# Softmax maxima from pairs of PSUM banks: one 1024-key reduction in place of two of 512 keys

## The chip, the cores and the metric

The kernel runs on one core of one Trainium2 chip. The metric is device time in microseconds (us) for one execution of the whole program, loads and stores included. Three executions of the kernel before took 2044.47, 2052.12 and 2060.83 us, so the median is 2052.12 us.

Five engines matter, each with its own queue worked in order: TensorE (PE in the profile; its weight loads are listed as PEld), VectorE (DVE), ScalarE (ACT), GpSimd (POOL) and SyncE (SP), which here only starts transfers. Matrix products land in PSUM, which holds eight banks of 512 float32 values per partition. Engines wait for each other through semaphores.

## What is computed

Two attention layers over one sequence of 2048 rows of width 512, 32 heads of 16, and a gated sum of the two:

```
q, k, v = split(x @ wqkv)                       # layer A: every row attends to all 2048 rows
a = softmax(q k^T / 4) v @ wo
# layer B: four segments of 512 rows; inside a segment causal attention,
# between segments a running memory (phi(x) = x+1 for x > 0, else exp(x))
p = softmax(q_s k_s^T / 4 + mask); a_dot = p v_s
a_mem = (phi(q_s) M) / (phi(q_s) z + 1e-6)
M = M + phi(k_s)^T v_s ; z = z + sum(phi(k_s))
b = (sigmoid(beta) a_mem + (1 - sigmoid(beta)) a_dot) @ wo_B
out = g * a + (1 - g) * b ,  g = sigmoid(sum(x * gate_w))
```

The softmax needs the maximum of each row of scores. The kernel computes those maxima exactly, in a pass of their own, before it computes the scores that go into the exponential.

## The kernel before

**Stages.** The first stage projects x to q, k and v of both layers (`qk_tile`, `v_tiles`, tiles `pr`) and builds B's memory (`mem_q`, `mem_k`). Then comes the main loop over 512 steps of layer A and 128 steps of layer B, and after it a tail that finishes the last output rows. A unit is (layer, group of 4 heads, chunk of 512 query rows). A unit of A has 16 steps, one for each block of 128 keys, a unit of B has 4. B's steps have 512, 384, 256 and 128 query columns, because of the causal mask.

**A step of the main loop** emits four score products (`score_parts`, L579, into tiles `st`, three banks; one bank holds one head, or two heads when they have at most 256 columns), the exponentials on ACT (L582), and the products with v of an earlier step (`values`, L601, into the one bank `ops`; in A they come in two halves, so that a step has two half steps). Beside them it emits the maxima of a unit that comes 22 steps later (in B 12 to 20): `max_parts`. In A each step has four products of 128 queries by 512 keys (L197, tiles `sm`), and after each one a maximum on DVE (L199, out to `pm`). A score product and a maximum product use different rows of the array and run side by side. In B a step has 4 products of 512 or of 384 keys, one to a bank, or 4 of 256 or of 128, two to a bank (L210); DVE adds the mask in place and takes the maximum (L215, one custom operation and one that reads its accumulator).

**Behind a unit's last maximum,** `finish_max` joins the partial maxima (`nm`, L162 on DVE; L164 in B), splits them into two parts on POOL (L168, L169), and three steps later `transpose_max` transposes them on PE (L175, tile `mt_ps`), copies them on ACT (L177) and sends them by DMA into the rows 48 and 49 of the q tile, where the score products pick them up.

**Beside the main loop** run the reciprocals of the softmax sums (L623 on DVE, four to a group), their loads and stores, and, in B, the output products: `out_products` (L747, tile `fin`) multiplies finished rows by the output weights. 24 products of 512 columns make one block of 128 output rows; they are hung on the ends of the steps of B in groups of three to five (`filler`). The copy L750 on ACT empties `fin`, and a DMA stores the rows.

**PSUM before.** `sm_ps` has three single banks for the whole program. In the main loop there are beside it three `st` banks, one `ops` bank and one bank `ms_ps`, which takes A's transpositions and, in B, `fin`; B's transpositions take their turn among the `sm` banks.

**Order.** The order of the instructions on every engine is the order in which the Python code emits them (`manual_schedule`). The framework adds the semaphore waits, from the tiles that an instruction reads and writes.

Of the kernel before, what the change touches and what calls it, by code (L numbers as in the profile page):

```python
# [10 lines left out]
F32 = mybir.dt.float32  # L11
F32R = mybir.dt.float32r
AF = mybir.ActivationFunctionType
ALU = mybir.AluOpType
AX = mybir.AxisListType
PSUM = bass.MemoryType.PSUM
# [3 lines left out]
D = 512  # L20
H = 32
DH = 16
CH = 512
# [17 lines left out]
def gated_mix(ctx, tc, x, xT, wqkv, a_wo, b_wq, b_wk, b_wv, b_wo, beta, gate_w, out):  # L41
    nc = tc.nc
# [55 lines left out]
    qp = ctx.enter_context(tc.tile_pool(name="qp", bufs=6))  # L98
    kp = ctx.enter_context(tc.tile_pool(name="kp", bufs=1))
    mp = ctx.enter_context(tc.tile_pool(name="mp", bufs=2))  # L100
    sm_ps = ctx.enter_context(tc.tile_pool(name="sm_ps", bufs=3, space=PSUM))

    units = [("A", g, c) for g in range(NG) for c in range(NCH)]
    units += [("B", g, c) for c in range(NCH) for g in range(NG)]
# [4 lines left out]
    nA = NG * NCH * 16  # L109

    qt, kt_, ktr = {}, {}, {}
# [8 lines left out]
    for i in range(8):  # L120
        t = kp.tile([128, 2, CH], F32R, name=f"k{i}")
# [28 lines left out]
    def rows(t, h, n):  # L150

        return t[64 * (h // 2):64 * (h // 2) + n, h % 2]


    pmt = {}
# [13 lines left out]
        nc.gpsimd.tensor_sub(ms[:, :, 1], nv, ms[:, :, 0].bitcast(F32))  # L169
        return ms  # L170

    def transpose_max(u, ms, pool, tag):

        pt = pool.tile([128, CH], F32, tag=tag, name="mt_ps")
        nc.tensor.matmul(pt[:32, :128], ms.rearrange("p r a h s -> p (r a h s)"), identr, start=True, stop=True)  # L175
        mt = mp.tile([32, 128], F32R, tag="mt", name="mt")
        nc.scalar.copy(mt, pt[:32, :128])  # L177
        for r in range(2):
            nc.sync.dma_start(raw(qt[u])[64 * r + 48:64 * r + 50], raw(mt)[16 * r:16 * r + 16])

    def max_parts(m):

        u, i = steps[m]
        side, g, c = u
        if i == 0:
            pmt[u] = mp.tile([128, 4, 4, 4 if side == "A" else 1], F32, tag="pm" + side, name="pm")
        pm = pmt[u]
        q = qt[u]

        share = {}  # L190

        def part(j):
            if side == "A":

                ps = sm_ps.tile([128, CH], F32, tag="sm", name="sm")
                h, s, kc = (2 if j < 2 else 0) + i // 8, i // 2 % 4, 2 * (i % 2) + j % 2
                nc.tensor.matmul(ps, rows(q[:, :, s * 128:(s + 1) * 128], h, 48), rows(kt_[side, g, kc], h, 48),  # L197
                                 start=True, stop=True)
                nc.vector.tensor_reduce(pm[:, h, s, kc:kc + 1], ps, axis=AX.X, op=ALU.max)  # L199
                return  # L200

            s = 3 - i
            n = (s + 1) * 128
            per = 2 if n <= 256 else 1
            h = (2, 3, 0, 1)[j]
            if j % per == 0:
                share["ps"] = sm_ps.tile([128, CH], F32, tag="sm", name="sm")
            ps = share["ps"]
            n0 = j % per * n
            nc.tensor.matmul(ps[:, n0:n0 + n], rows(q[:, :, s * 128:(s + 1) * 128], h, 48),  # L210
                             rows(kt_[side, g, c][:, :, :n], h, 48), start=True, stop=True)
            if j % per == per - 1:
                for e in range(per):
                    r = ps[:, e * n:(e + 1) * n]
                    nc.vector.tensor_tensor_reduce(r, r, cmask[:, CH - n:], 1.0, -3.0e38, ALU.add, ALU.max,  # L215
                                                   pm[:, h - per + 1 + e, s, 0:1])
        return [lambda j=j: part(j) for j in range(4)]
# [4 lines left out]
            ms = finish_max(u)  # L222
            late.append((m + LATE_T, u, ms))

    def run_late(pool, tag, every=False):
        for e in [e for e in late if every or e[0] < mnext[0]]:
            late.remove(e)
            transpose_max(e[1], e[2], pool, tag)

    loaded = [0]  # L230

# [16 lines left out]
    with ExitStack() as p0:  # L248
# [6 lines left out]
        st = p0.enter_context(tc.tile_pool(name="st", bufs=1))  # L255
        pr_ps = p0.enter_context(tc.tile_pool(name="pr_ps", bufs=3, space=PSUM))
        me_ps = p0.enter_context(tc.tile_pool(name="me_ps", bufs=2, space=PSUM))

# [209 lines left out]
        def some_max(place):  # L470
            if not parts:
                if mnext[0] == LEAD_A:
                    return
                loads(mnext[0] + PRE)
                parts.extend(max_parts(mnext[0]))

            parts.pop(0)()
            parts.pop(len(parts) // 2)()
            if not parts:
                after_max(mnext[0])  # L480
                mnext[0] += 1
                run_late(me_ps, "me")

        s0 = now[0]
        for k in range(NCH):
# [37 lines left out]
    hl = ctx.enter_context(tc.tile_pool(name="hl", bufs=2, reuse_waits="tile"))  # L523
    st_ps = ctx.enter_context(tc.tile_pool(name="st_ps", bufs=3, space=PSUM, reuse_waits="tile"))
    o_ps = ctx.enter_context(tc.tile_pool(name="o_ps", bufs=1, space=PSUM, reuse_waits="tile"))
    ms_ps = ctx.enter_context(tc.tile_pool(name="ms_ps", bufs=1, space=PSUM, reuse_waits="tile"))

    ops = o_ps.tile([128, CH], F32, name="ops")
    nc.vector.memset(ops, 0.0)
# [84 lines left out]
    held = {}  # L614
# [120 lines left out]
            eng.tensor_sub(l[:, os], t, held["hi", side, c, b][:, os].bitcast(F32))  # L735
        held["lo", side, c, b] = l

    def out_products(c, b, n0, n1, pool, tag):
        if n0 == 0:
            held["ps", c, b] = pool.tile([128, D], F32, tag=tag, name="fin")  # L740
        ps = held["ps", c, b]
        for n in range(n0, n1):
            side = "AB"[n // 12]
            half, o = n % 12 // 4, n % 4
            l = held["lo" if half == 0 else "hi", side, c, b]
            r = wos[side][1 if half == 1 else 0]
            nc.tensor.matmul(ps, l[:, o], r[:, o], start=(n == 0), stop=(n == 23))  # L747
        if n1 == 24:
            t = fr.tile([128, D], F32, tag="res", name="res", bufs=2)
            nc.scalar.copy(t, ps)  # L750
            nc.sync.dma_start(out[c * CH + b * 128:c * CH + (b + 1) * 128, :], t)
# [13 lines left out]
    for c in range(1, NCH):  # L765
        t0 = 24 * c
# [21 lines left out]
    def filler(t, f):  # L788
        fill.setdefault(t, []).append(f)

    for c in range(NCH - 1):
        base = nA + (c + 1) * 32
        apart = 7 if c < NCH - 2 else 5
        per = -(-24 // apart)
        at(base + 3, lambda c=c: b_invert_load(c))
        for i in range(4):
            at(base + 6 + i // 2, lambda c=c, i=i: recip(("B", c), i))
        at(base + 7, lambda c=c: b_invert(c))
        for i, os in enumerate(((0, 1), (2, 3))):
            at(base + 6 + i, lambda c=c, os=os: raw_load(c, os))  # L800
            at(base + 8 + i, lambda c=c, os=os: am_load(c, os))
            at(base + 10 + i, lambda c=c, os=os: inv_load(c, os))
            at(base + 12 + i, lambda c=c, os=os: at_load(c, os))
        for b in range(4):
            t0 = base + 14 + apart * b
            at(t0, lambda c=c, b=b: out_mul(c, b))
            at(t0 + 1, lambda c=c, b=b: out_add(c, b))
            at(t0 + 2, lambda c=c, b=b: out_hi(c, b, "B"))
            at(t0 + 3, lambda c=c, b=b: (out_lo(c, b, "B", nc.gpsimd), out_hi(c, b, "A")))
            at(t0 + 4, lambda c=c, b=b: out_lo(c, b, "A", nc.gpsimd))  # L810
            for n in range(24):
                filler(t0 + 5 + n // per, lambda c=c, b=b, n=n: out_products(c, b, n, n + 1, ms_ps, "ms"))


    nS = len(steps)
# [6 lines left out]
    for t in range(nS):  # L822
        for f in beside.get(t, []):
            f()
        side = steps[t][0][0]

        ms_list = []
        while mnext[0] < nS and mnext[0] - lead(mnext[0]) <= t:
            ms_list.append(mnext[0])
            mnext[0] += 1  # L830
        mm = []
        for m in ms_list:
            loads(m + PRE)
            mm += max_parts(m)
        ss = score_parts(t)
        per = -(-len(mm) // 4) if mm else 0
        waiting.append(t)
        lag = LAG_A if side == "A" else LAG_B

        done = [w for w in waiting if w <= t - lag]  # L840
        del waiting[:len(done)]
        for h in range(4):
            for w in done if side == "A" and h == 2 else []:
                values(w, 0)
            for w in done if side == "B" and h == 3 else []:
                values(w)
            ss[h]()
            for f in mm[h * per:(h + 1) * per]:
                f()
        for w in done if side == "A" else []:  # L850
            values(w, 1)
        for m in ms_list:
            after_max(m)

        run_late(*((ms_ps, "ms") if t < nA else (sm_ps, "sm")), every=not ms_list)
        for f in fill.get(t, []):
            f()
    for t in waiting:
# [10 lines left out]
    for b in range(4):  # L869
        out_hi(c, b, "A")  # L870
        out_lo(c, b, "A", nc.vector)
        out_products(c, b, 0, 12, *((sm_ps, "sm") if b < 3 else (st_ps, "st")))
    for b in range(5):
        if b < 4:
            out_mul(c, b)
            out_add(c, b)
            out_hi(c, b, "B")
        if b:
            out_lo(c, b - 1, "B", nc.vector)
            out_products(c, b - 1, 12, 24, None, None)  # L880


def build():
# [32 lines left out]
```

## Time and profile before

| | |
|---|---|
| executions, median (lowest to highest) | 2052.12 us (2044.47 to 2060.83) |
| profiled execution: time, span of its instructions | 2040.8 us, 2039.1 us |
| mean granted TensorE clock in it | 0.953 of full speed |
| busy in the span: PE, DVE, ACT, POOL | 2001.6, 1688.3, 1478.2, 212.0 us |
| main loop, layer A's steps | from about 335 to 1630 us |
| main loop, layer B's steps | from about 1630 to 1998 us |

The profile is of one execution, on its slowest core, which here is the only one. A line "L199 DVE ..." is a group of instructions of line 199 of the program. Out <- in are the program's tile names, the number after x is the count; behind it stand the busy time in us and the mean duration of one in ns. Because instructions overlap on an engine, the busy time of a group can be less than count times mean. "Idle before" is what the engine idled just before these instructions, with the work that ended the idling. Matmuls are pipelined and their ends are modelled, so that PE can read as busy while it isn't at its peak; start to start distances are the safer reading. PEclk is the share of the TensorE clock that was granted.

### The profile page before, as it was taken

The page shows a single profiled execution, that of the slowest core. Times are in us where ns is not written, and L with a number is a line of the kernel's source. Part 1 is how long each engine was busy: PE and PEld are TensorE (multiplying, and loading weights), DVE is VectorE, ACT ScalarE, POOL GpSimd, SP SyncE. Part 2 cuts the span into 40 slices and gives each one's busy share as a digit, 9 for nine tenths or more (in the row PEclk, how much of TensorE's full clock was granted, in tenths as well). Part 3 has the DMA queues.
Part 4 walks back from the last instruction along what each step waited for, and adds up shares of the span by engine and source line. Part 5 has one row for each costly group of instructions (what it writes and reads, how often), then busy time and mean ns, then how long its engine had stood idle before and what let it go on. Part 6 is the DMA issues. An engine that isn't in the chain of part 4 may idle for free.

```text
span 2039.1 us, 41498 instructions
## 1 busy us (share of the span) xinstructions
PE 2001.6 (98%) x16113; PEld 912.9 (45%) x16113; DVE 1688.3 (83%) x3476; ACT 1478.2 (72%) x2823; POOL 212.0 (10%) x372
## 2 busy tenths in 40 slices
PE   8999999999999999999999999999999999999998
PEld 6887665333333333333333333333333344454545
DVE  3235896999999899999999999999998567787842
ACT  3234334888888788888888888888888855565652
POOL 3000000021200100000010000010000023343330
PEclk9999999999999899999999999999999955698989
DMA  6667434032400410110221111130103144546542
GB/s 225 216 232 241 166 141 150 31 100 94 138 15 26 93 44 26 38 35 26 59 66 39 30 30 38 32 94 15 38 15 75 54 121 138 150 146 180 163 132 91
DMA packets 94725, 190.69 MB, mean 94 GB/s; under 512 B 15888, under 2 KB 30000, under 8 KB 91712
## 3 DMA queue, kind: packets, MB, share of 16 engines
q1 hardware_dynamic: 93536, 187.30, 30.6%
q8 instruction: 127, 2.08, 0.4%
q0 software_dynamic: 992, 0.74, 0.2%
q14 instruction: 70, 0.57, 0.1%
HBM read 111.94 MB, written 74.86 MB: 92 GB/s over the span
## 4 chain that ended last, share of the span: by engine, by line
PE 86%; DVE 5%; DMA 4%; ACT 3%; issue 1%; SPq 1%; DVEq 0%; ACTq 0%
PE st L579 35%; PE ops L601 31%; PE pr L274 12%; PE fin L747 4%; DVE pm L199 3%; PE sm L197 2%; ACT p L582 2%; PE sm L210 2%; DMA qA<-mt 1%; ACT oraw L608 1%; DVE sm L215 1%; PE num L422 1%; DMA inv<-rdB 1%; PE mt_ps L175 1%; SPq L694 0%
## 5 line engine op out<-in xcount | busy, mean ns | idle before, releaser
L582 ACT ACTIVATE p<-st 128x512 f32<-128x512 f32 (+2 forms) x2432 | 1298.2, 585 | 301.0 <-PE sm L210 120.8
L199 DVE TENSOR_REDUCE pm<-sm 128x1 f32<-128x512 f32 x2048 | 1254.5, 684 | 31.2 <-PE sm L197 25.1
L579 PE MATMUL st<-qA,k 50*128 50x512 f32 x2048 | 751.4, 447 | 7.7 <-DMA qA<-mt 4.8
L197 PE MATMUL sm<-k,qA 48*128 48x512 f32 x2048 | 751.6, 451 | 0.7 <-DVE pm L199 0.5
L601 PE MATMUL ops<-p,vA 128*17 128x256 f32 x8176 | 645.5, 388 | 5.7 <-ACT oraw L608 5.6
L579 PEld LDWEIGHTS st<-qA,k 50*128 50x128 f32 x2048 | 303.4, 185 | 433.2 <-ACT p L582 411.2
L215 DVE CUSTOM_DVE_ANT_0 sm<-sm,cmask 128x256 f32<-128x256 f32 (+3 forms) x512 | 244.0, 512 | 104.7 <-PE sm L210 81.4
L197 PEld LDWEIGHTS sm<-k,qA 48*128 48x128 f32 x2048 | 310.6, 185 | 24.9 <-DVE pm L199 12.4
L601 PEld LDWEIGHTS ops<-p,vA 128*17 128x17 f32 x8176 | 135.7, 95 | 367.6 <-issue 347.4
L210 PE MATMUL sm<-k,qB 48*128 48x256 f32 (+3 forms) x512 | 183.7, 446 | 5.3 <-DVE pm L215 2.8
L579 PE MATMUL st<-qB,k 50*128 50x256 f32 (+3 forms) x512 | 174.0, 441 | 0.8 <-ACT p L582 0.2
L579 PEld LDWEIGHTS st<-qB,k 50*128 50x128 f32 x512 | 100.4, 235 | 133.5 <-issue 63.1
L168 POOL CAST ms<-nm 128x16 fp32r<-128x16 f32 x64 | 14.1, 220 | 1200.3 <-DVE nm L162 1150.0
L601 PE MATMUL ops<-p,vB 128*17 128x512 f32 (+3 forms) x1024 | 121.6, 556 | 0.0
L323 DVE TENSOR_TENSOR q<-pr,q 128x512 fp32r<-128x512 f32 x64 | 44.0, 687 | 88.0 <-ACT q L316 84.7
L210 PEld LDWEIGHTS sm<-k,qB 48*128 48x128 f32 x512 | 101.8, 233 | 14.7 <-DVE pm L215 9.8
L584 POOL TENSOR_SCALAR_AFFINE_SELECT p<-p 128x512 f32<-128x512 f32 x128 | 82.8, 647 | 244.2 <-ACT p L582 244.2
L316 ACT CAST q<-pr 128x512 fp32r<-128x512 f32 x64 | 37.4, 585 | 82.8 <-PE pr L274 65.6
L215 DVE DVE_READ_ACCUMULATOR2_ANT pm<- 128x1 f32 x512 | 72.2, 141 | 0.1
L274 PE MATMUL pr<-xh,wql 128*128 128x512 f32 x128 | 55.5, 434 | 8.0 <-ACT xh L367 6.0
L274 PE MATMUL pr<-xl,wqh 128*128 128x512 f32 x128 | 51.5, 402 | 0.0
L274 PE MATMUL pr<-xh,wqh 128*128 128x512 f32 x128 | 51.2, 400 | 0.0
(137 smaller groups left out, 1258.4 us busy)
## 6 DMA issues: line engine op xcount, KB each, us to landing
qdA<-q SPq DMA_DIRECT2D x32, 256.0 KB
kdA<-q SPq DMA_DIRECT2D x32, 256.0 KB
qdB<-q SPq DMA_DIRECT2D x32, 256.0 KB
k<-kdA SPq DMA_DIRECT2D x64, 128.0 KB
kdB<-q SPq DMA_DIRECT2D x32, 256.0 KB
qA<-qdA SPq DMA_DIRECT2D x64, 128.0 KB
odA<-oraw SPq DMA_DIRECT2D x32, 256.0 KB
k<-kdB SPq DMA_DIRECT2D x64, 128.0 KB
```

What stands on the lines that cost most here:

```text
L197: nc.tensor.matmul(ps, rows(q[:, :, s * 128:(s + 1) * 128], h, 48), rows(kt_[side, g, kc], h, 48), start=True, stop=True)
L199: nc.vector.tensor_reduce(pm[:, h, s, kc:kc + 1], ps, axis=AX.X, op=ALU.max)
L210: nc.tensor.matmul(ps[:, n0:n0 + n], rows(q[:, :, s * 128:(s + 1) * 128], h, 48), rows(kt_[side, g, c][:, :, :n], h, 48), start=True, stop ...
L215: nc.vector.tensor_tensor_reduce(r, r, cmask[:, CH - n:], 1.0, -3.0e38, ALU.add, ALU.max, pm[:, h - per + 1 + e, s, 0:1])
L274: nc.tensor.matmul(ps, l(a, k), r(b, k), start=(n == 0), stop=(n == 11))
L316: nc.scalar.copy(q1, ps)
L323: nc.vector.tensor_sub(q2, ps, q1.bitcast(F32))
L579: nc.tensor.matmul(ps[:, h % per, :n], rows(k[:, :, b * 128:(b + 1) * 128], h, 50), rows(q[:, :, q0:], h, 50), start=True, stop=True)
L582: nc.scalar.activation(p[:, h - per + 1:h + 1, :n], ps[:, :, :n], AF.Exp, scale=SCALE)
L584: nc.gpsimd.affine_select(out=p[:, :, 0:128], in_=p[:, :, 0:128], pattern=[[0, 4], [1, 128]], base=0, channel_multiplier=-1, compare_op=AL ...
L601: nc.tensor.matmul(ops[32 * h:32 * h + 17, q0 + a:q0 + b], v[h], p[:, h, a:b], start=(i == 0 and a == 0), stop=(i == last and b == n), til ...
L747: nc.tensor.matmul(ps, l[:, o], r[:, o], start=(n == 0), stop=(n == 23))
```

## The change

The four maxima of a step of A come in two pairs: the two products of a half step now go to the two banks of one tile of 1024 values, and one DVE operation takes the maximum over both banks (L226 in the changed file). There are two such tiles, `smT[0]` and `smT[1]`, used in turn. The partial maxima of a unit shrink from four to two per row. The first 22 steps of maxima, which run beside the projections, keep the old form (the five removed lines of the diff, with a tile of `me_sm`) with three banks of their own, and their `pm` is filled by POOL beforehand.

B's maxima take the banks `smT[0][:, 0]`, `smT[0][:, 1]` and `smT[1][:, 0]` in turn. The fourth, `smT[1][:, 1]`, takes `fin`. All transpositions of maxima in the main loop take an `st` bank. The bank `ms_ps` is gone, so that all eight banks stay in use: 4 `smT`, 3 `st`, 1 `ops`. In the tail the four last `fin` take the four `smT` banks.

```diff
@@ pools @@
-    sm_ps = ctx.enter_context(tc.tile_pool(name="sm_ps", bufs=3, space=PSUM))
+    smT = []
+    pairs = [0]
+    singles = [0]
+    def pair_banks():
+        pairs[0] += 1
+        return smT[(pairs[0] - 1) % 2]
+    def single_bank():
+        singles[0] += 1
+        i = (singles[0] - 1) % 3
+        return smT[i // 2][:, i % 2]
...
+        me_sm = p0.enter_context(tc.tile_pool(name="me_sm", bufs=3, space=PSUM))
...
-    ms_ps = ctx.enter_context(tc.tile_pool(name="ms_ps", bufs=1, space=PSUM, reuse_waits="tile"))
+    sm_ps = ctx.enter_context(tc.tile_pool(name="sm_ps", bufs=1, space=PSUM, reuse_waits="tile"))
+    smT += [sm_ps.tile([128, 2, CH], F32, name=f"sm{i}") for i in range(2)]
@@ max_parts @@
         if i == 0:
-            pmt[u] = mp.tile([128, 4, 4, 4 if side == "A" else 1], F32, tag="pm" + side, name="pm")
+            width = 1 if side == "B" else 2 if smT else 4
+            pmt[u] = mp.tile([128, 4, 4, width], F32, tag="pm" + side + str(width), name="pm")
+            if not smT:
+                nc.gpsimd.memset(pmt[u], -3.0e38)
...
             if side == "A":
-                ps = sm_ps.tile([128, CH], F32, tag="sm", name="sm")
-                h, s, kc = (2 if j < 2 else 0) + i // 8, i // 2 % 4, 2 * (i % 2) + j % 2
-                nc.tensor.matmul(ps, rows(q[:, :, s * 128:(s + 1) * 128], h, 48), rows(kt_[side, g, kc], h, 48),
-                                 start=True, stop=True)
-                nc.vector.tensor_reduce(pm[:, h, s, kc:kc + 1], ps, axis=AX.X, op=ALU.max)
+                if not smT:
+...
+                    return
+                if j % 2 == 0:
+                    share["ps"] = pair_banks()
+                ps = share["ps"]
+                h, s, e = (2 if j < 2 else 0) + i // 8, i // 2 % 4, i % 2
+                nc.tensor.matmul(ps[:, j % 2], rows(q[:, :, s * 128:(s + 1) * 128], h, 48),
+                                 rows(kt_[side, g, 2 * e + j % 2], h, 48), start=True, stop=True)
+                if j % 2:
+                    nc.vector.tensor_reduce(pm[:, h, s, e * pm.shape[3] // 2:][:, 0:1], ps, axis=AX.XY, op=ALU.max)
                 return
...
             if j % per == 0:
-                share["ps"] = sm_ps.tile([128, CH], F32, tag="sm", name="sm")
+                share["ps"] = single_bank()
@@ transpose_max, out_products and their callers @@
-        pt = pool.tile([128, CH], F32, tag=tag, name="mt_ps")
+        pt = bank()
...
-            held["ps", c, b] = pool.tile([128, D], F32, tag=tag, name="fin")
+            held["ps", c, b] = bank()
...
-                filler(t0 + 5 + n // per, lambda c=c, b=b, n=n: out_products(c, b, n, n + 1, ms_ps, "ms"))
+                filler(t0 + 5 + n // per, lambda c=c, b=b, n=n: out_products(c, b, n, n + 1, lambda: smT[1][:, 1]))
...
-        run_late(*((ms_ps, "ms") if t < nA else (sm_ps, "sm")), every=not ms_list)
+        run_late(lambda: st_ps.tile([128, CH], F32, tag="st", name="mt_ps"), every=not ms_list)
...
-        out_products(c, b, 0, 12, *((sm_ps, "sm") if b < 3 else (st_ps, "st")))
+        out_products(c, b, 0, 12, lambda: single_bank() if b < 3 else smT[1][:, 1])
```

## The prediction

> **What bounds the kernel now.** I read the busy shares first, then the chain that ended last, the costliest groups, the busy times by stage, and the rows of single steps. All durations are from the profiled execution (time 2040.8 us, span 2039.1, so 1.7 lie around the span); the median of the runs shown is 2052.1, 11.3 higher, inside a spread of 16.4. I work out a difference against the profiled execution and add it to the median.
>
> ```profile
> PE 2001.6 (98%) x16113; PEld 912.9 (45%) x16113; DVE 1688.3 (83%) x3476; ACT 1478.2 (72%) x2823; POOL 212.0 (10%) x372
> ...
> PE 86%; DVE 5%; DMA 4%; ACT 3%; issue 1%; SPq 1%; DVEq 0%; ACTq 0%
> ...
> L199 DVE TENSOR_REDUCE pm<-sm 128x1 f32<-128x512 f32 x2048 | 1254.5, 684 | 31.2 <-PE sm L197 25.1
> ```
>
> The chain is 86% PE and 5% DVE. But the average hides two stages. Busy time of PE, PEld, DVE, ACT and POOL, then granted clock, in most of A and in two stretches of B:
>
> ```profile
> 335.00:1568.00 1233.00, 1219.49 (x11761) 444.57 (x11760) 1209.28 (x2023) 1082.72 (x2024) 60.96 (x107) 0.99 0.19 50
> ...
> 1624.40:1720.00 95.60, 95.28 (x502) 42.23 (x500) 62.59 (x252) 49.89 (x109) 28.00 (x50) 0.50 0.45 125
> ...
> 1774.00:1849.00 75.00, 74.66 (x522) 38.31 (x520) 59.47 (x227) 46.89 (x102) 28.33 (x47) 0.97 0.52 156
> ```
>
> In A, PE and DVE are both full (1219 and 1209 of 1233 us), so busy time can't say which paces. Single rows can. First an A half step around a `nm`, then two half steps at the end of A, where no maxima are left:
>
> ```profile
> 1209.00 0.22 DVE L162 TENSOR_REDUCE nm<-pm 128x16 f32<-128x64 f32 x1
> 1209.14 5.46 DVE L199 TENSOR_REDUCE pm<-sm 128x1 f32<-128x512 f32 x9
> ...
> 1209.47 0.49 PE L579 MATMUL st<-qA,k 50*128 50x512 f32 x1
> ...
> 1210.87 0.49 PE L579 MATMUL st<-qA,k 50*128 50x512 f32 x1
> ...
> 1599.80 0.73 PE L579 MATMUL st<-qA,k 50*128 50x512 f32 x2
> 1601.02 0.73 PE L579 MATMUL st<-qA,k 50*128 50x512 f32 x2
> ```
>
> A half step without maxima takes 1601.02 − 1599.80 = 1.22 us; a plain one with maxima also takes 1.22 (1208.25 to 1209.47). So PE paces A: two score products at 0.33 each and 0.55 of values. DVE only keeps up: 5.46/9 = 0.607 a maximum, two in 1.214; where it catches up, it goes at 0.598, 1.196 a half step. It has 20 ns to spare, so whatever else it does delays PE: the half step behind `nm` takes 1210.87 − 1209.47 = 1.40, 0.18 more.
>
> **The change in A.** Removed: 1960 maxima at 0.598 to 0.608 in the main loop. Added: 980 over 1024 keys, which no row shows. The mask-and-maximum of B (L215) goes from 0.515 at 384 keys to 0.649 at 512, 1.047 ns a key; so the second 512 keys cost 0.536, and the pair 0.598 + 0.536 = **1.134 us**. Lower bound 1024 x 1.047 = 1.07 (no fixed part), upper 1.196 (no part shared). I take 1.134, since the 512-key reduction itself is the nearest row. All three lie under 1.22: nothing is gained on a plain half step. What is gained is slack, 0.02 to 0.15 (0.08 likeliest) a half step, in which DVE catches up.
> - `nm`: 30 x 0.18 = 5.3 us. A pair tile is needed again two half steps after its filling began (2.44 us), and its maximum would end at about 0.85 + 1.13 = 2.0; 0.4 to spare covers the 0.32 that `nm` takes. All goes: −5.3.
> - The reciprocals (L623, six groups in A): steps that hold them run over by 5.8 us in all. A group is four reciprocals at 0.34 and a product at 0.29, 1.7 together; 0.4 spare and 0.08 a half step recover part. I take half, −2.5; bounds 0 and −5.8.
> - Kept: each unit's wait for the copy out of `ops` (0.27) and the PE time of its transposition (0.17). The transposition now takes an `st` bank; the next score product for that bank needs an exponential that by the rows is done 0.08 earlier: 0. If that cover is gone, 31 x 0.1 = 3.
> - The transition: the new pair tiles wait for the banks of the projections, but PE already waits there for the exponential of the first step (2.3 us of idle, to 339.2): 0. The two `memset`s of `pm` on POOL run before the main loop, ahead of work that waits anyway: 0.
>
> A: **−8** (0 to −11).
>
> **The change in B.** Reductions there keep their form and take three banks as before. But the fourth bank, `fin`, is half of `smT[1]`, whose other half takes every third single. Waits follow tiles: DVE adds the mask in place, so a group of `fin` products behind such a single waits until DVE has taken that maximum, though it lies in the other bank. In before, `fin` had its own tile. PE works in order, so scores and values queued behind `fin` wait too. A unit of B has 12 singles, so always the same ones fall on `smT[1]`: the third of the 512-key step, the second of 384, the first of 256, the last of 128. One unit in the rows of before:
>
> ```profile
> 1819.51 1.19 PE L747 MATMUL fin<-wohA,hA 128*128 128x512 f32 x4
> 1820.37 0.14 DVE L215 DVE_READ_ACCUMULATOR2_ANT pm<- 128x1 f32 x1
> ...
> 1822.71 1.20 PE L747 MATMUL fin<-wohB,lB 128*128 128x512 f32 x4
> 1823.11 0.14 DVE L215 DVE_READ_ACCUMULATOR2_ANT pm<- 128x1 f32 x1
> ...
> 1825.35 0.14 DVE L215 DVE_READ_ACCUMULATOR2_ANT pm<- 128x1 f32 x1
> 1825.50 1.19 PE L747 MATMUL fin<-wolB,hB 128*128 128x512 f32 x4
> ...
> 1827.92 1.14 PE L747 MATMUL fin<-wohB,hB 128*128 128x512 f32 x4
> 1828.07 0.14 DVE L215 DVE_READ_ACCUMULATOR2_ANT pm<- 128x1 f32 x1
> ```
>
> Each wait is end of the read + 0.054 (DVE to PE wherever DVE releases PE in this trace) − start of `fin`: 128: 1820.37 + 0.14 + 0.054 − 1819.51 = 1.05; 512: 0.60; 384: 0.05; 256: 0.34. Over the 12 such units (48 groups; the last chunk's `fin` have no maxima beside them) the same subtraction gives 12.8 + 6.5 + 0.7 + 4.3 = **24.3 us**.
>
> Likewise a single on `smT[1]` waits for the ACT copy of `fin` (L750, 0.59) where it comes soon after: by the rows 0 to 0.8 for the eight blocks, +3. In the tail two `fin` wait for a copy of the block in the other half of their tile: +1.6. B's transpositions wait for `st` exponentials instead of `sm` maxima; waits around them are 9.4 us now, and about the same ends then: 0 (bounds ±4).
>
> Absorbed: where PE waits for other things now, a `fin` wait ahead of it costs nothing. But in the two stretches with `fin` and maxima (1774 to 1942 without the 17 us between them) PE is dense:
>
> ```profile
> PE sm L210 <- DVE pm L215: 1.1, 3, 0.5
> PE sm L210 <- ACT mt L177: 0.6, 1, 0.6
> ```
>
> These are all of PE's waits there (us in total, times, longest): 1.7 us in 151. I take −1.7; the weight loads also wait for DVE and ACT, 4.7 us, and if PE's busy rows hide that much, −6.4. The other way, the first weight load behind a `fin` wait is no longer covered: 0.06 for each of 48, up to +3; I take +1.5. Lower bound of all B: 0, if DVE's order shifts so that every maximum is taken ahead of its `fin`.
>
> B: 24.3 + 3 + 1.6 − 1.7 + 1.5 = **+28.7** (0 to +36). With A's −7.8: **+21**.
>
> **The rivals.**
> - *DVE paces A.* For it: DVE is busy 1209 of 1233 us. Against: the 1.22 us half steps without maxima. If so, every half step falls from 1.217 to 1.134: 980 x 0.083 = −81, with B's +29 in place of A's −8 near −52: 2000. The Trainium skill ("Trainium Kernel Development and Optimization", Performance Expectations) calls matmul busy time a bad metric, since matmuls are pipelined, and lets occupancy count for other engines; by that, DVE's 98% in A would name the bound. The trace disagrees here, by those half steps.
> - *The `fin` waits are hidden* (the one near zero): DVE gets its maxima earlier, or the waits fall where PE would wait anyway, and A's −8 is left: 2044. It decides if they total under 8 us. For it: in the rows above two of the four waits are under 0.35, less than one mask-and-maximum. Against: PE's 1.7 us of waits, and that a later PE makes the maxima later too.
> - *The clock* (slower by more): the dense `fin` stretches hold the clock at 0.97, the sparser ones before at 0.50, and a unit takes 11.2 us there with `fin`, against 12.3 without at half clock. If the waits break up the fill so that the 151 us of it (1774 to 1849 and 1866 to 1942) go at 0.85, B gets some 20 us more (151 x 0.97 / 0.85 − 151 = 21): 2093. It decides if the idle time of some windows falls just where the grant is set: in A an idle of 2.4 us at 700 us cost 10 us at half clock, idles of 1.2 and 1.7 cost none; the new ones are 1.1 at most, but come often. The Trainium skill ("TensorE: Matmul & The Clock Gate", A second HAM failure mode) tells of a kernel whose cycling through PSUM queues made PE idle briefly so often that its clock swung between half and full; by that rule this rival would be the result. The trace agrees only in part: in B the clock does swing.
>
> **How the numbers follow.** One per cent, 20 us, is about what a measurement of this kernel can tell from no change. Forecast +21 (from +12 to +30): 2052 + 21 = **2073**, chance 0.53; the clock (+41, 2093) 0.26; hidden (−8, 2044) 0.15; DVE paces 0.06. Slower by over 1%: 0.26 and half of 0.53, 0.53. Faster: 0.06. Within 1%: the rest, 0.41. The range runs from the hidden case at 2044 to the clock case with 9 us of its own spread, 2102; DVE's case and the clock's far end are left out.
>
> **What would show it.** Right: in A, L226 starts 1.13 us apart where it catches up and has idle time between (DVE about 1111 + 15 of 1290 us, not 98%); the half step behind `nm` takes 1.22; plain steps stay at 2.44. In B, PE and PEld of `fin` wait for DVE by 20 to 30 us in all, ahead of the 128 and 512 groups most, and units with `fin` take about 13 us at full clock. Wrong: plain steps of 2.3 us in A (DVE paced); no wait of `fin` on DVE (hidden); 1774 to 1942 granted under 0.9 (clock); L226 at 1.2 (nothing shared: `nm` is then not covered, and A gains 0). The sum's weakest term is the 24.3 us: it is read off an order of work that the change itself shifts.

## The result, and the profile after

Four executions of the changed kernel took 2237.95 us at the median (2213.98 to 2269.13), against 2050.55 of the kernel before beside it: a ratio of **1.087**, 95% interval 1.0755 to 1.0984. Ratios, here and below, leave out slow executions (here the one of 2269.13), so they are not quite the quotients of the medians. The forecast was 2073, with a range up to 2102. The profiled execution took 2247.06 us, its span is 2245.3, and the mean granted clock is 0.886 in place of 0.953.

The page of the changed kernel, busy shares, chain and the new maxima:

```profile
PE 2146.3 (96%) x16113; PEld 954.0 (42%) x16113; DVE 1692.5 (75%) x2496; ACT 1487.4 (66%) x2823; POOL 213.7 (10%) x374
...
PE 85%; DVE 6%; DMA 3%; ACT 3%; issue 1%; SPq 1%; DVEq 0%; ACTq 0%
...
L226 DVE TENSOR_REDUCE pm<-sm 128x1 f32<-128x1024 f32 x980 | 1185.3, 1222 | 30.3 <-PE sm L223 29.4
```

The chain is the same mixture as before, and DVE's busy time rose by 4 us. Averages over the program do not show where 206 us of span came from. Cutting the traces at the score products that begin a unit does (us; the tail begins at the last score product; "own banks" is the second run of the first experiment below):

| stretch | before | after | own banks |
|---|---|---|---|
| up to A's first score product | 335.1 | 334.7 | 334.6 |
| A, units 0 to 29 | 1208.0 | 1205.7 | 1207.6 |
| A, units 30 and 31 | 79.0 | 111.7 | 79.1 |
| B, units 0 to 11 (no `fin` yet) | 139.6 | 192.8 | 118.2 |
| B, units 12 to 31 | 233.5 | 354.1 | 221.4 |
| tail | 44.0 | 46.3 | 44.1 |

A is as fast as before until B's maxima begin beside its last two units. All of the loss starts there. Busy times by stage of the changed kernel (PE, PEld, DVE, ACT, POOL, then granted clock): most of A, B's units before `fin`, and B's units with `fin`:

```profile
335.00:1568.00 1233.00, 1218.51 (x11781) 432.62 (x11780) 1196.19 (x1044) 1084.61 (x2029) 61.34 (x109) 0.99 0.19 50
...
1680.00:1845.00 165.00, 143.24 (x654) 61.92 (x654) 90.13 (x341) 67.05 (x140) 35.03 (x64) 0.50 0.41 110
...
1845.00:2190.00 345.00, 309.49 (x1447) 147.70 (x1449) 167.97 (x595) 141.01 (x297) 87.72 (x135) 0.66 0.33 97
```

In B PE is busy for 87 to 90% of the time where it had 98%. The clock is 0.50 throughout the first stretch and 0.66 in the second. Over units 0 to 11 and 12 to 31 of the kernel before it was 0.58 and 0.89, so that the first stretch had run mostly at half clock already. PE's waits in B (us in total, times, longest):

```profile
PE sm L237 <- DVE pm L242: 42.7, 64, 1.4
PE sm L776 <- DVE pm L242: 12.0, 15, 1.0
```

L776 are the `fin` products (named after their tile, `sm`); their waits were forecast. L237 are **B's own maximum products**, and they wait more than three times as long. One such wait in rows, where the first three of four products of 512 keys go to the three banks in turn:

```profile
1729.70 1.16 PE L608 MATMUL st<-qB,k 50*128 50x512 f32 x2
1731.76 0.97 PE L237 MATMUL sm<-k,qB 48*128 48x512 f32 x2 [0.90 <-DVE pm L242]
...
1731.57 0.14 DVE L242 DVE_READ_ACCUMULATOR2_ANT pm<- 128x1 f32 x1
```

The first maximum product had started with the score product at 1729.70 (in a row, left out here, that begins with the product before it). The second goes to the other bank of the same tile, and starts at 1731.76, just after DVE has read the accumulator of the first (1731.57 + 0.14 = 1731.71, plus the 0.054 that DVE to PE takes). It waits for the maximum of the product directly before it, although nobody uses its bank. The corresponding rows of the kernel before:

```profile
1694.17 0.73 PE L210 MATMUL sm<-k,qB 48*128 48x512 f32 x1
1694.70 0.62 PE L579 MATMUL st<-qB,k 50*128 50x512 f32 x1
1694.70 0.63 PE L210 MATMUL sm<-k,qB 48*128 48x512 f32 x1
```

There the second product starts 0.53 us behind the first (this is at half clock) and side by side with the second score product. So the change costs PE twice: it waits, and the maximum product then runs behind the score product in place of beside it.

### The profile page after: what moved, and what is told of

The parts are those of the page before. It is cut to its first block, busy times and chain, and to the rows that moved or that the text cites. A ratio compares the mean times of both kernels' runs of the same rounds, so it can differ in the third digit from the quotient of the medians.

```text
span 2245.3 us, 40529 instructions
## 1 busy us (share of the span) xinstructions
PE 2146.3 (96%) x16113; PEld 954.0 (42%) x16113; DVE 1692.5 (75%) x2496; ACT 1487.4 (66%) x2823; POOL 213.7 (10%) x374
## 4 chain that ended last, share of the span: by engine, by line
PE 85%; DVE 6%; DMA 3%; ACT 3%; issue 1%; SPq 1%; DVEq 0%; ACTq 0%
PE st L608 33%; PE ops L630 31%; PE pr L302 9%; PE sm L776 5%; DVE sm L242 4%; PE sm L237 4%; ACT p L611 1%; DMA qA<-mt 1%; PE sm L215 1%; ACT oraw L637 1%; DMA raw<-xT 1%; DVE pm L242 1%; PE sm L223 1%; PE num L450 1%; DMA qdA<-q 0%
## 5 line engine op out<-in xcount | busy, mean ns | idle before, releaser
L226 DVE TENSOR_REDUCE pm<-sm 128x1 f32<-128x1024 f32 x980 | 1185.3, 1222 | 30.3 <-PE sm L223 29.4
L608 PE MATMUL st<-qA,k 50*128 50x512 f32 x2048 | 767.5, 455 | 6.9 <-DMA qA<-mt 5.9
L223 PE MATMUL sm<-k,qA 48*128 48x512 f32 x1960 | 722.3, 448 | 1.7 <-ACT gt L536 1.7
L223 PEld LDWEIGHTS sm<-k,qA 48*128 48x128 f32 x1960 | 293.1, 186 | 3.2 <-ACT gt L536 2.0
L237 PE MATMUL sm<-k,qB 48*128 48x256 f32 (+3 forms) x512 | 224.5, 536 | 52.9 <-DVE pm L242 47.1
L608 PE MATMUL st<-qB,k 50*128 50x256 f32 (+3 forms) x512 | 216.0, 507 | 0.3 <-ACT p L611 0.3
L608 PEld LDWEIGHTS st<-qB,k 50*128 50x128 f32 x512 | 120.3, 275 | 151.1 <-issue 105.0
L237 PEld LDWEIGHTS sm<-k,qB 48*128 48x128 f32 x512 | 116.9, 272 | 106.8 <-DVE pm L242 104.3
L630 PE MATMUL ops<-p,vB 128*17 128x512 f32 (+3 forms) x1024 | 141.1, 640 | 0.0
L217 DVE TENSOR_REDUCE pm<-sm 128x1 f32<-128x512 f32 x88 | 56.5, 683 | 12.6 <-PE sm L215 11.5
```

The lines of the kernel that those rows point to most:

```text
L223: nc.tensor.matmul(ps[:, j % 2], rows(q[:, :, s * 128:(s + 1) * 128], h, 48), rows(kt_[side, g, 2 * e + j % 2], h, 48), start=True, stop=True)
L226: nc.vector.tensor_reduce(pm[:, h, s, e * pm.shape[3] // 2:][:, 0:1], ps, axis=AX.XY, op=ALU.max)
L608: nc.tensor.matmul(ps[:, h % per, :n], rows(k[:, :, b * 128:(b + 1) * 128], h, 50), rows(q[:, :, q0:], h, 50), start=True, stop=True)
L630: nc.tensor.matmul(ops[32 * h:32 * h + 17, q0 + a:q0 + b], v[h], p[:, h, a:b], start=(i == 0 and a == 0), stop=(i == last and b == n), til ...
```

## The experiments

Times are medians of runs beside the kernel before on the same chip, and ratios are to that.

**Own banks.** `smT` is given up at B's first maximum, and four tiles of one bank each take its place.

```diff
+    def b_banks():
+        if not own:
+            sm_stack.close()
+            own_ps = ctx.enter_context(tc.tile_pool(name="own_ps", bufs=1, space=PSUM, reuse_waits="tile"))
...
+            own.extend([o0, o1, o2, o3])
+        return own
...
-        return smT[i // 2][:, i % 2]
+        return b_banks()[i]
...
-                filler(t0 + 5 + n // per, lambda c=c, b=b, n=n: out_products(c, b, n, n + 1, lambda: smT[1][:, 1]))
+                filler(t0 + 5 + n // per, lambda c=c, b=b, n=n: out_products(c, b, n, n + 1, lambda: b_banks()[3]))
```

> The changed kernel, but when A's maxima are done the two pair tiles are given up and B gets four tiles of one bank each: three for its maxima in turn, one for fin, so no two of them share a tile. Theory T (the loss is in B: banks that share a tile make PE wait for the maximum of the product just before, and PE's idling halves the clock): nearly all of the loss goes; what stays is A's gain and the transpositions in the st ring, so 2038 to 2052 us against 2050 before, -0.6% to 0. Rival R (the loss comes from the transpositions in the st ring or from the passage from A to B): still over 2150. Rival C (the pairs in A): the same, over 2150.

Measured: 2014.96 us, ratio **0.9865** (0.9832 to 0.9898), and the whole loss is gone, so rivals R and C fall. It is also faster than the kernel before, by more than theory T allowed; how far that can be explained stands further down. The same kernel run again on another chip:

> Own banks once more, on the same chip as the one-line kernel, to price the pairs against it. By the unit lengths of A (0.13 us in each unit) and the wait behind the long loads, own banks is 3 to 8 us below the one-line kernel; if the pairs are worth nothing, the two agree within 3 us.

2012.77 us, ratio 0.9866 (0.9826 to 0.9907). The one-line kernel that this expectation compares it with comes below.

**Which sharing.** Two kernels put back one of the two shared tiles each.

```diff
-            o0 = own_ps.tile([128, CH], F32, name="o0")
-            o1 = own_ps.tile([128, CH], F32, name="o1")
+            o0 = own_ps.tile([128, 2, CH], F32, name="o0")
...
-            own.extend([o0, o1, o2, o3])
+            own.extend([o0[:, 0], o0[:, 1], o2, o3])
```

> As own banks, but the first and second bank of B's maxima are halves of one tile; the third and fin have tiles of their own. T: most of the loss is here, 2170 to 2230 us. If the fin waits of the forecast are the loss: 2045 to 2060.

Measured: 2213.90 us, 1.0824 (1.0793 to 1.0856). The shared tile of the first two maxima banks alone makes nearly the whole loss, as T said. PE's largest wait from 1610 us on, 43.0 us of it in B (the tiles are called `o` here); the same wait is 3.2 us in all in own banks:

```profile
PE o L249 <- DVE pm L254: 44.5, 73, 1.2
```

The other kernel lets the third bank and `fin` share, as `o2[:, 0]` and `o2[:, 1]`:

> As own banks, but the third bank of B's maxima and fin are halves of one tile; the first and second have tiles of their own. This is the sharing that the forecast costed alone: by its sum 29 us above own banks, 2068 to 2080 us. T as it stands gives the same if the clock holds, and 2090 to 2120 if the fin waits lower the clock.

Measured: 2038.42 us, 0.9985 (0.9957 to 1.0012). Against own banks that is a factor of 1.012, 24 us; the forecast's sum for this sharing was 28.7. (The expected range of the time itself, 2068 to 2080, was missed, since own banks is that much faster than T had it.) The waits of `fin` products in its trace:

```profile
PE o L789 <- DVE pm L254: 20.2, 36, 1.0
```

20.2 us over 36 waits, where the subtraction in the rows of before had given 24.3 over 48 of which 12 were close to nothing. And the clock held: 0.97 over its units with `fin`. In the 13 units with `fin` that run at full clock both here and in the second run of own banks, this sharing costs 1.64 us a unit, 28 us if the 17 units from 12 to 28 are like these (an estimate).

**Fewer banks, none of them next to each other.**

```diff
-        i = (singles[0] - 1) % 3
-        return smT[i // 2][:, i % 2]
+        i = (singles[0] - 1) % 2
+        return smT[i % 2][:, 0]
```

> The changed kernel, but B's maxima take only two banks in turn, the first halves of the two tiles; the second half of the first tile stays empty, fin keeps the second half of the second (the four tail blocks take the four banks). So there is one bank less, but a product never waits for the maximum of the product just before it, only for the one before that, as every second one's tile is the other. T: faster than the changed kernel, 2080 to 2190 us. If the number of banks decides: slower than the changed kernel, over 2240.

Measured: 2236.63 us, 1.0955 (1.0919 to 1.0991): no better than the changed kernel, so as a forecast of the total T missed. By stretches it is two effects. Without `fin`, two banks are better than three halves in two tiles: B's units 0 to 11 take 174.6 us against 192.8 (14.73 a unit against 16.45, at the same clock of 0.50), and A's units 30 and 31 82.3 against 111.7. With `fin` they are worse, 394.8 against 354.1: now every second maximum falls into `fin`'s tile, and its waits grow.

```profile
PE sm L776 <- DVE pm L242: 42.6, 49, 1.0
PE sm L237 <- DVE pm L242: 7.5, 24, 0.6
```

**Waits or clock.** The changed kernel, with each score product of B's first 12 units issued twice:

```diff
+            for _ in range(2 if nA <= t < nA + 48 else 1):
                 nc.tensor.matmul(ps[:, h % per, :n], ...
```

> The changed kernel, but in the first 12 units of B (before any fin) every score product is issued twice into the same bank, so that PE has 16 more products of 128 to 512 columns a unit. It tells the waits from the clock. If the half clock is a large part of the loss: the added work fills PE's waits and holds the clock, the granted clock there goes from 0.51 to over 0.9 and a unit from 16.45 us to 12 to 14.5, so 2180 to 2220 us in all. If the waits alone make the loss, or idling at these places keeps the clock low anyway: a unit stays at 16.4 or gets longer, 2235 to 2280 us.

Measured: 2247.58 us, 1.1028 (1.0965 to 1.1091), as the second of the two expectations has it; it does not tell apart the two causes that this one names. A unit takes 18.28 us in place of 16.45. The clock did not move, though PE is now busy for 92% of the stretch:

```profile
1690.00:1790.00 100.00, 92.07 (x447) 49.17 (x447) 50.28 (x188) 38.60 (x78) 21.55 (x37) 0.50 0.36 99
```

Own banks with the same doubling:

> Own banks, with the doubled score products in the first 12 units of B. Own banks has some of these units at half clock (12.09 us) and some at full clock (8.85). If PE's load sets the clock and the added work hides: all at full clock, 105 to 118 us for the 12 instead of 122, 2000 to 2012 in all. If the added work is on the path: units of 10 to 13 us, 2015 to 2045.

2018.04 us, 0.9884 (0.9854 to 0.9914), not to be told from own banks. In its trace the first 12 units do run at full clock for the most part, but a unit then takes 9.19 us where own banks has 8.85 at full clock, and the 12 units make 117.8, as much as there.

So the split between waits and clock is read from units at equal clock. At 0.50, a unit without `fin` takes 12.09 in own banks and 16.45 in the changed kernel: 4.36 of waits and lost overlap, 52 us over 12 units. At 1.00, units 22, 23 and 25 take 14.03, 14.88 and 13.28 in the changed kernel and 10.41, 11.32 and 9.99 in own banks: 3.5 each, 60 us if all 17 units with maxima beside them (12 to 28) are like these (an estimate; unit 30, without maxima, takes 11.46 and 11.45). That is 112 of the 207 us that the two traces differ by in B; the other 95, by the same estimate, are units that run at half clock where own banks runs them at full.

The 32 us in A's last two units are nearly all clock. The clock falls to half at 1596 us, with PE still busy for 96% of the time:

```profile
1612.00:1652.00 40.00, 38.44 (x195) 12.58 (x194) 14.20 (x49) 18.62 (x36) 0.42 (x2) 0.50 0.14 35
```

A plain half step then takes 2.13 us in place of 1.22, as it does in the kernel before at half clock (703 to 711 us). For the 32 half steps of unit 31 that makes 29 us, and the unit is 30 longer; PE's waits for B's maxima in units 30 and 31 are 4.4 us in all. So it is shown that the sharing of the first two banks lowers the clock: both kernels that have it without doubled products fall to half at 1596 to 1598 us, while before and own banks stay at full until 1624 or later. By what way so little waiting does that is not shown.

**Why own banks is faster than before.** Three kernels take one difference each. First, B's transpositions go back to a turn among the maxima's banks:

```diff
-        run_late(lambda: st_ps.tile([128, CH], F32, tag="st", name="mt_ps"), every=not ms_list)
+        run_late((lambda: st_ps.tile(...)) if t < nA else single_bank, every=not ms_list)
```

> Own banks, but B's transpositions take their turn among the three banks of B's maxima again, as in the kernel before; so only layer A is changed. If moving the transpositions to the st ring is what makes own banks faster in B: its first 12 units go back from 122 to about 140 us and the time to 2034 to 2044, within 0.5% of before. If the gain is A's: it stays at 2012 to 2020.

2044.02 us, 1.0017 (0.9991 to 1.0043). The gain is gone, so it is not in A. B's first 12 units take 141.2 us, most of them 12.53 at half clock, where own banks has 12.09 at half clock. Second, the reverse: the kernel before with this one line changed.

```diff
-        run_late(*((ms_ps, "ms") if t < nA else (sm_ps, "sm")), every=not ms_list)
+        run_late(*((ms_ps, "ms") if t < nA else (st_ps, "st")), every=not ms_list)
```

> The kernel before with one line changed: B's transpositions take an st bank instead of a turn among the banks of B's maxima. No pairs, no shared tiles. If this alone is what makes own banks faster: a ratio to before of 0.984 to 0.992, units of B at full clock of 8.85 us instead of 10.05. If it needs the pairs or the other banks as well: 0.995 to 1.002.

2027.94 us, **0.9929** (0.9896 to 0.9962): faster, about half of own banks' gain; the ratio lies between the two expectations and the interval touches both. Its units at full clock take 8.85 as expected. The 10.05 of the kernel before is no like measure, as that unit had a clock of 0.84 and none of the first 12 ran at full clock. Own banks on this chip is 15 us faster, more than the 3 to 8 expected. Third, own banks with A's maxima by 512 keys again, in four single banks:

```diff
-        return smT[(pairs[0] - 1) % 2]
+        return smT[(pairs[0] - 1) % 4]
...
-                    nc.vector.tensor_reduce(pm[:, h, s, e * pm.shape[3] // 2:][:, 0:1], ps, axis=AX.XY, op=ALU.max)
+                nc.vector.tensor_reduce(pm[:, h, s, 2 * e + j % 2:][:, 0:1], ps, axis=AX.X, op=ALU.max)
```

> Own banks, but A's maxima are taken by 512-key operations again, one for each of four single banks in turn (before: three); B as in own banks. It undoes the pair operation alone. If the pair operation is worth what the unit lengths show (0.13 us in each of 31 units, and part of the reciprocals): 4 to 9 us over own banks, 2018 to 2026. If four banks give the same slack as the pair: no difference, 2012 to 2018.

2018.57 us, 0.9906 (0.9874 to 0.9937); the interval overlaps that of own banks. The unit lengths of A are sharper than the times: a plain unit takes 39.63 before and 39.63 in the one-line kernel (both three banks), 39.50 in the changed kernel and own banks (pairs), and 39.49 here (four banks, no pairs). So the **fourth bank** is enough for A's small gain; the pair operation adds nothing to it that these units show.

Last, own banks with all four banks for maxima until the first `fin`:

> Own banks, but until the first fin B's maxima take all four banks in turn. If PE in B's first 12 units still waits for a bank: 2 to 15 us below own banks. If three banks of their own are enough: the same within 4 us.

2017.14 us, 0.9885 (0.9849 to 0.9922): no gain to be seen against own banks, although undisturbed units at full clock shorten from 8.85 to 8.34.

What stays open is the size of the one line's gain against that of own banks. Executions of one kernel spread along their mean granted clock: the 17 of the kernel before beside the first experiment fall on a line of 13 us for each 0.01. Read at a clock of 0.97 on such lines, before is at 2017 to 2022 (three sets, an estimate, since its executions reach 0.963 at most), the one-line kernel at 2022, own banks at 2015 and 2016. At equal clock, then, 1 to 7 us of own banks' gain of some 28 are left, and none of the one line's. So nearly all of the gain goes with the clock that an execution gets: on average 0.953 to 0.956 before, 0.966 with the one line, 0.968 and 0.973 in own banks, and 0.951 where the transpositions go back. That the transposition's place changes it is shown; by what way it does is not.

## Why the prediction was wrong

**The direction** was right and the size was not: 2238 against 2073, outside the range of 2044 to 2102. The direction was luck, too: the kernel with `fin`'s sharing alone, which is what the forecast costed, ran at 0.9985 of before, since the moved transpositions gain about what it loses.

**The step that failed** is the first sentence on B: "Reductions there keep their form and take three banks as before." They take three banks, but the first and second are halves of one tile. The forecast stated the rule that matters (waits follow tiles), applied it to the fourth bank, and not to the first two. Their sharing alone gave 1.0824 to before, which is 1.097 over own banks, `fin`'s alone 1.012 over own banks. The rows of before would have told it. The second product of 512 keys starts at 1694.70, as shown above, and this is the read of the first one's accumulator:

```profile
1696.09 0.14 DVE L215 DVE_READ_ACCUMULATOR2_ANT pm<- 128x1 f32 x1
```

The same subtraction, 1696.09 + 0.14 + 0.054 − 1694.70, gives a wait of 1.58 us at this one place of a unit. The forecast put such waits at nothing. The trace has 42.7 us of them in B, and by the estimates above the sharing costs some 112 us there in waits and lost overlap, `fin`'s part included, and as much again in units at half clock.

**`fin`'s waits:** right in mechanism and in size. 24.3 us forecast and 20.2 in the trace; 28.7 for the sharing in all and 24 measured, or 28 by the units at full clock.

**A:** forecast −8. Units 1 to 29 took 1157.8 us in place of 1164.2, −6.4. The half step behind `nm` fell from 1.39 to 1.22 as forecast; these are the rows of the changed kernel, where consecutive half steps start 1.22 apart on both sides of `nm`:

```profile
1206.61 0.18 DVE L175 TENSOR_REDUCE nm<-pm 128x16 f32<-128x32 f32 x1
...
1206.92 0.49 PE L608 MATMUL st<-qA,k 50*128 50x512 f32 x1
...
1208.14 0.49 PE L608 MATMUL st<-qA,k 50*128 50x512 f32 x1
```

But the reason given for it, that the pair operation is shorter, is not what decides: 512-key operations in four banks give the same 1.22. The three units with the first reciprocals fell from 40.5 to 39.6 or 39.7, all that they had over. The passage into A (unit 0, 43.75 before and 47.89 after) was costed at 0; the kernel before with one line of B changed has 46.92 there, so this need not be the change's.

**PE paces A:** right. Plain half steps stayed at 1.22 us. The rival in which DVE paces falls, and with it, for this kernel, the reading by occupancy that the Trainium skill allows for engines other than TensorE ("Trainium Kernel Development and Optimization", Best Practices): DVE was busy for 1209 of 1233 us in A and did not pace it.

**The pair's price:** forecast 1.134 with bounds 1.07 and 1.196. Of the 980, 73 start 1.10 to 1.15 apart and 17 less than 1.10, where DVE catches up. But the idle time that the forecast expected on DVE does not show: in step with PE the operations start 1.22 apart, and their rows last 1.22 as well.

**The clock:** named as a rival, for a wrong trigger. `fin`'s waits alone left it at 0.97. With the first two maxima banks shared it is 0.50 in the first stretch and 0.66 in the second, or 0.75 there where they alone share. The idle at 700 us that the rival quotes as 2.4 us is 2.00 in PE's rows. The rule of the Trainium skill ("TensorE: Matmul & The Clock Gate", A second HAM failure mode) that frequent brief idling of PE makes its clock swing fits the changed kernel's units with `fin`, where it goes from 0.50 to 1.00 and back. It does not tell why the clock stays at 0.50 through the first stretch, also with doubled products and a PE busy for 92%, and for 95.60 us of the kernel before, with PE busy for 95.28 of them.

**B's transpositions:** costed at 0 with bounds of ±4. Moving them is worth −0.7% in the kernel before, a real gain that the changed kernel hides under its loss. What failed is "about the same ends then": it compared the waits at the transposition alone. With the transpositions among the maxima's banks a unit at half clock takes 0.44 us more (12.53 against 12.09), some 5 us over 12 units; the rest goes with the clock.

**Absorption:** 1.7 us was right to be small; the hidden rival falls.

## What to carry to other kernels

Before two buffers are put into one tile, look at what the waits are attached to: with three halves in two tiles a unit took longer (16.45 us) than with two banks in two tiles (14.73). When a rule on waits is found for one part of a change, apply it to every product that writes such a tile, also to those whose code is the same as before. A saturated engine's busy share is no measure of its slack, and a spare bank can give what a faster operation was meant to.

## What the runs showed of the hardware that was not expected

- A row of the 1024-key maximum lasts 1.22 us when its start is paced by PE and starts follow by 1.08 to 1.13 when it isn't, so that a row's length overstates what the operation needs.
- Short idles of PE go before a halved clock. From 365 to 1560 us of the thirteen traces here, eight idles of 0.78 to 1.43 us left it at full; of 31 from 1.62 to 2.68 us, 26 were followed by 3.4 to 17.1 us at half clock, and it fell nowhere else in these stretches.
- The granted clock stays at half under a PE that the rows show as fully busy. Own banks, a stretch at half clock and one shortly after it, with the same code:

```profile
1655.00:1705.00 50.00, 49.82 (x272) 22.46 (x272) 35.09 (x142) 27.00 (x59) 17.41 (x29) 0.50 0.58 159
1708.00:1750.00 42.00, 39.32 (x308) 18.73 (x308) 38.71 (x159) 28.80 (x66) 13.57 (x29) 0.98 0.62 170
```

  A unit takes 12.09 us in the first and 8.85 in the second. What made the clock rise at about 1709 us no run here tells.
- Of the spread of some 1% between executions of one kernel, most goes with the mean granted clock, 13 to 16 us for each 0.01 in the three sets of the kernel before.
